# A transformer block on one core: 12 corrections to the list scheduler's order in place of 67

## The chip, the core and the metric

The kernel runs on one core of a Trainium2 chip. The core has five engines, each with an instruction queue of its own that it works through strictly in order: TensorE (PE in the profile; PEld is its loading of weights), VectorE (DVE), ScalarE (ACT), GpSimd (POOL) and SyncE (SP), which here only issues DMA transfers. An instruction that needs the result of another engine waits at the head of its queue, and everything behind it waits too. The metric is the device time of the whole program in microseconds. The kernel before takes 846.68 us, the median of three runs (845.99 to 846.89).

## What is computed

One block of a transformer in float32: LayerNorm, attention over a dilated window, a residual, LayerNorm, a SwiGLU feed-forward network (FFN), a residual. The sizes are 2048 rows (S), model width 640 (D), inner width 1728 (F), and 32 heads of 20. Each position attends to itself and to the seven positions 2, 4, ... 14 before it. Cut to what matters:

```python
def _A_ref(x, wqkv, wo):
    H = 32; Dh = D // H; W, dil = 8, 2
    qkv = (x @ wqkv).reshape(B, S, 3, H, Dh).transpose(2, 0, 3, 1, 4)
    q, k, v = qkv[0], qkv[1], qkv[2]
    idx = jnp.arange(S)[:, None] - (jnp.arange(W) * dil)[None, :]
    mask = idx >= 0
    kg, vg = (the rows idx of k and of v)
    logits = jnp.einsum("bhsd,bhswd->bhsw", q, kg) * Dh ** -0.5
    attn = _softmax(jnp.where(mask[None, None], logits, -1e9))
    o = jnp.einsum("bhsw,bhswd->bhsd", attn, vg)
    return o.transpose(0, 2, 1, 3).reshape(B, S, D) @ wo

def _B_ref(x, w_gate, w_up, w_down):
    return (_silu(x @ w_gate) * (x @ w_up)) @ w_down

h = x + _A_ref(_layernorm(x), wqkv, wo)
h2 = h + _B_ref(_layernorm(h), w_gate, w_up, w_down)
```

## The kernel before

**Tiling.** The 2048 rows are four blocks b of 512, each held as four row tiles j of 128 rows. Heads are taken in four groups g of eight. The FFN's inner width is 14 column tiles i (i0 to i12 of 128, i13 of 64). Products of full float32 accuracy are made of three passes: each operand is split into a high part (a cast on ScalarE) and a low part (a subtraction on VectorE), and TensorE adds high·high, low·high and high·low. So nearly every operand of TensorE first passes through ScalarE and then VectorE.

**Stages.** First come the projections to q, k and v (L552) and the attention of all blocks and groups (L594 loads, L601 and L636 products, L608, L619 and L644 sums on VectorE, L621 the exponential). For each block follow the output projection `wo` (L768 to L805), LayerNorm (L315 to L383, its square root at L373 and what follows it at L374), the FFN with its loads (L845, L851, L858), casts (L846, L847), projections `proj` (L869 to L871), down products `downs` (L880 to L896) and gates (L903 to L915), and `finish` (L1160 to L1182), which adds the down products to the rows `h` and stores them (L1182). The attention of later blocks runs on VectorE while TensorE does FFN and output projection of earlier ones. Blocks 2 and 3 share the products of their FFN through combinations of their columns (L964 products, L1060 to L1130 sums); one factor of it is kept in a tile `kept` (L1130, L1144), which lies in the buffer that held the upper half of `h` before. In the output projection each row tile takes two halves of 320 columns; for blocks 1 and 2 all of them go through a single bank, which ScalarE empties (L802).

**The order.** The program is not executed as it is written. Every piece of work is put on a list by `Plan.add(engine, cost, function, reads, writes, priority)`, 2739 numbered operations in all; `Plan.add` works out from the memory ranges which earlier operations each depends on. `Plan.order` then plans them like a list scheduler: each engine takes the ready operation of the best priority, with estimated costs, and so each operation gets a planned start. The final order is a heap over the dependences with the planned start as its key, to which `SHIFT` adds a correction in microseconds for single operations, by number (L38 and the key in `order`):

```python
key = [(t + SHIFT.get(n, 0.0), n) for n, t in enumerate(start)]
heap, out = [key[n] for n in range(len(ops)) if not left[n]], []
while heap:
    n = heapq.heappop(heap)[1]
    out.append(n)
```

A positive number puts an operation back in its engine's queue, a negative one brings it forward, as far as its dependences let it. Each engine then executes its operations in this order. The waits between engines are put in from the memory ranges. An operation may be several instructions.

**The operations that are spoken of**, with the engine, the line, and the time at which the operation began in the profiled execution of before:

| operation | engine, line | what | at us |
|---|---|---|---|
| 47, 68, 131, 139 | DVE L516, ACT L526, PE L554 | first block: columns of LayerNorm, a cast of weights, two q/k/v products | 14.4, 14.8, 11.6, 13.9 |
| 989 | DVE L374 | LayerNorm's scale after the square root, block 3 | 229.0 |
| 1649, 1650 | PE L871 | FFN block 1, projections of i9, first two steps | 486.9, 488.1 |
| 1662 | PE L896 | FFN block 1, a down product | 494.2 |
| 1453, 1455, 1459 | PE L800 | `wo` of block 2: row tile 2 (two halves), row tile 3 | 500.0, 504.5, 507.4 |
| 1653, 1654 | PE L871 | FFN block 1, further projections of i9 | 502.2, 503.4 |
| 1659, 1679, 1660 | PE L896 | FFN block 1, down products | 532.3 (1659), 506.7 (1660) |
| 820, 825 | DVE L675 | transposes of the attention's result, block 3 | 508.7, 509.1 |
| 1696 | DVE L904 | gate of i11, block 1 | 531.0 |
| 1769, 1771, 1773, 1775 | SP L1182 | stores of block 1's four row tiles | 633.1, 704.4, 676.7, 686.6 |
| 2212 | DVE L1130 | first write of `kept` | 707.0 |

Of the kernel before, what the change touches and what calls it, by code (L numbers as in the profile page):

```python
# [35 lines left out]
PR = {'x': 0.5, 'yst': 8, 'yld': 2, 'wqd': 4, 'wqh': 0.5, 'wql': 4, 'qev': 1, 'kvs': 0.4, 'atl': 1.2, 'exp': 0.5, 'ost': 3, 'wod': 2, 'woh': 8, 'wol': 1.2, 'old': 1.5, 'fld': 4, 'lst': 6, 'wev': 1.5, 'fh': 2.2, 'fl': 8, 'ln1': 8, 't1': 1, 'wo0': 1.2, 'wo': 2.2, 'ln1t': 1.2, 'xb': 0.4, 'tr': 10, 't1t': 2.2, 'ln1d': 0.5, 'hst': 10, 'hld': 10, 'ht': 1, 'hc': 2, 'jd': 3, 'jp': 8, 'js': 4, 'jl': 0.4, 'ja': 0.5, 'jfld': 1.2, 'jfh': 4, 'jfl': 1, 'jhi': 4, 'jmu': 0.4, 'jlo': 0.9, 'jcm': 0.5, 'w3': 1, 'w3e': 8, 'w3o': 0.4, 'w3x': 8, 'w3l': 2.2, 'jy': 6}  # L36

SHIFT = {  # L38
# [8 lines left out]
}  # L47


# [1285 lines left out]
```

## Time and profile before

The profiled execution took 846.34 us; the part that the profile shows, its span, is 844.2 us.

| | us |
|---|---|
| median of the runs | 846.68 |
| profiled execution | 846.34 |
| its span | 844.2 |
| TensorE busy | 837.7 |
| VectorE busy | 706.9 |
| ScalarE busy | 405.0 |
| GpSimd busy | 23.6 |

The granted clock of TensorE is 1.00 in all stretches of the span. A row of a timeline reads: start and length in us, engine, line, instruction, the tile it writes and the tiles it reads with their shapes, and the number of instructions put together in the row; in brackets follows how long the engine stood idle before it and what it waited for. `bank` is an accumulator in PSUM, `fa`, `ra`, `sha` and `shb` are large tiles in SBUF that hold many smaller ones, `acts` holds the gated FFN columns and `h` the rows. SPq is SyncE's queue, where a transfer's issue is shown and not its flight.

### The profile page before, as it was taken

The numbers are of one execution on the slowest core, as the hardware profiler recorded it, in microseconds if no ns is written. First come the engines' busy times: TensorE is split into PE (matmuls) and PEld (weight loads), VectorE is DVE, ScalarE is ACT, GpSimd is POOL, SyncE is SP. The second block draws the span as 40 slices with busy tenths as digits, with TensorE's granted clock in tenths as the row PEclk, the third lists the DMA queues.
The fourth block names the chain that finished last, engine by engine and source line by source line (L and its number), as shares of the span: only waits on it lengthen the run. The fifth ranks groups of instructions, "written<-read, shape, count | busy, mean of one in ns | idle before, by whom it ended". The sixth has DMA issues, their size and how long they took to land.

```text
span 844.2 us, 10772 instructions
## 1 busy us (share of the span) xinstructions
PE 837.7 (99%) x3961; PEld 711.7 (84%) x3961; DVE 706.9 (84%) x841; ACT 405.0 (48%) x674; POOL 23.6 (3%) x33
## 2 busy tenths in 40 slices
PE   9999999999999999999999999999999999999998
PEld 7888888889888888888888898888888887888886
DVE  8899899999998999999999999999434986655652
ACT  6662563245663433875533466555447543333331
POOL 0000000000000100010000000000000000000000
PEclk9999999999999999999999999999999999999999
DMA  8887486567577779567886965876844564454432
GB/s 294 323 298 222 164 274 229 182 216 241 195 255 292 251 255 308 180 216 260 341 289 227 343 234 190 285 274 225 300 164 146 184 229 144 156 169 144 152 115 89
DMA packets 90260, 191.12 MB, mean 226 GB/s; under 512 B 31568, under 2 KB 50896, under 8 KB 89568
## 3 DMA queue, kind: packets, MB, share of 16 engines
q1 hardware_dynamic: 90208, 190.44, 65.8%
q8 instruction: 31, 0.51, 0.3%
q14 instruction: 21, 0.17, 0.1%
HBM read 144.26 MB, written 46.14 MB: 226 GB/s over the span
## 4 chain that ended last, share of the span: by engine, by line
PE 97%; DVE 2%; issue 1%; ACT 0%; DMA 0%; POOL 0%; SPq 0%; POOLq 0%
PE bank L552 25%; PE bank L880 21%; PE bank L869 21%; PE bank L964 17%; PE bank L799 8%; PE bank L986 2%; PE bank L445 1%; DVE fa L608 1%; PE bank L460 1%; DVE acts L915 0%; PE bank L513 0%; PE bank L1166 0%; PE bank L739 0%; DMA out_dram<-h 0%; PE bank L410 0%
## 5 line engine op out<-in xcount | busy, mean ns | idle before, releaser
L869 PE MATMUL bank<-shb,ra 128*128 128x512 f32 x810 | 189.9, 390 | 0.0
L869 PEld LDWEIGHTS bank<-shb,ra 128*128 128x128 f32 x810 | 151.6, 188 | 31.1
L880 PE MATMUL bank<-ra,acts 128*128 128x512 f32 (+1 forms) x662 | 163.1, 389 | 0.0
L880 PEld LDWEIGHTS bank<-ra,acts 128*128 128x128 f32 x662 | 122.5, 188 | 24.5
L552 PE MATMUL bank<-ra,sha 128*128 128x480 f32 x480 | 106.0, 380 | 0.3 <-ACT sha L515 0.3
L552 PE MATMUL bank<-ra,shb 128*128 128x480 f32 x470 | 102.8, 378 | 0.0
L552 PEld LDWEIGHTS bank<-ra,sha 128*128 128x128 f32 x480 | 89.5, 188 | 14.2 <-ACT sha L515 0.8
L552 PEld LDWEIGHTS bank<-ra,shb 128*128 128x128 f32 x470 | 88.0, 188 | 13.2
L636 DVE TENSOR_TENSOR fa<-fa 128x2560 f32<-128x2560 f32 x32 | 90.3, 2823 | 0.8
L601 DVE TENSOR_TENSOR fa<-fa 128x2560 f32<-128x2560 f32 x32 | 90.2, 2820 | 0.4
L608 DVE TENSOR_REDUCE fa<-fa 128x128 f32<-128x2560 f32 x32 | 90.0, 2812 | 0.5
L964 PE MATMUL bank<-shb,ra 128*128 128x512 f32 x360 | 88.3, 391 | 0.8 <-DVE fa L1102 0.8
L557 ACT ACTIVATE st<-bank,fa 128x480 f32<-128x480 f32 x64 | 41.7, 660 | 97.3 <-PE bank L552 86.9
L964 PEld LDWEIGHTS bank<-shb,ra 128*128 128x128 f32 x360 | 67.0, 188 | 14.7 <-DVE fa L1102 1.2
L644 DVE TENSOR_TENSOR fa<-fa 128x1280 f32<-128x1280 f32 (+2 forms) x68 | 75.9, 1116 | 1.6
L1102 DVE TENSOR_TENSOR fa<-bank,fa 128x512 f32<-128x512 f32 x60 | 41.2, 691 | 42.8 <-PE bank L964 41.8
L799 PE MATMUL bank<-ra 128*128 128x320 f32 x480 | 74.6, 309 | 0.0
L799 PEld LDWEIGHTS bank<-ra 128*128 128x128 f32 x480 | 72.3, 188 | 2.2 <-ACT fa L802 0.3
L964 PE MATMUL bank<-ra 128*128 128x512 f32 x288 | 68.4, 390 | 0.0
L964 PEld LDWEIGHTS bank<-ra 128*128 128x128 f32 x288 | 53.9, 188 | 11.7 <-ACT shb L1023 0.4
L846 ACT CAST ra<-fa 128x1280 fp32r<-128x1280 f32 (+1 forms) x38 | 45.8, 1206 | 22.5 <-PE bank L869 16.8
L914 ACT CAST acts<-fa 128x512 fp32r<-128x512 f32 x47 | 29.2, 621 | 54.4 <-DVE fa L904 28.0
(152 smaller groups left out, 842.4 us busy)
## 6 DMA issues: line engine op xcount, KB each, us to landing
fa<-in_ffn_dram SPq DMA_DIRECT2D x46, 960.0 KB, 7.0
ra<-lsc SPq DMA_DIRECT2D x45, 320.0 KB, 4.1
fa<-ksc SPq DMA_DIRECT2D x16, 880.0 KB, 5.3
fa<-vsc SPq DMA_DIRECT2D x16, 880.0 KB, 6.2
ra<-lsc SPq DMA_DIRECT2D x21, 640.0 KB, 5.2
lsc<-ra SPq DMA_DIRECT2D x13, 640.0 KB, 4.4
ksc<-st SPq DMA_DIRECT2D x16, 320.0 KB, 2.7
qsc<-st SPq DMA_DIRECT2D x16, 320.0 KB, 3.0
```

Of the source, the lines that this page charges most:

```text
L552: T.matmul(banks[bk][:, 0:480], l, r_(wq(g, w, c), 480), start=(p, c) == first_mm, stop=(p, c) == last_mm)
L557: P.add("ACT", act(480) + 0.06, lambda bk=bk, j=j: A.activation(stage_t()[:, so : so + 1920].rearrange("p (t j c) -> p t j c", t=3, j=NJ)[ ...
L601: P.add("DVE", dve(2560), lambda: V.tensor_tensor(f(PROD, 2560).rearrange("p (j w c) -> p j w c", j=2, w=W), window(ko, 2 * jp), f(qo + 32 ...
L608: P.add("DVE", dve(2560), lambda: V.tensor_reduce(f(lo + 128 * jp, 128), f(PROD, 2560).rearrange("p (n d) -> p n d", d=DH), axis=AX.X, op= ...
L636: V.tensor_tensor(f(PROD, 2560).rearrange("p (j w d) -> p j w d", j=2, d=DH), bass.AP(tensor=fa[:, vo : vo + 160].tensor, offset=fa[:, vo ...
L644: V.tensor_add(dst(v), v[:, :, 0:m, :], v[:, :, m : 2 * m, :])
L799: T.matmul(banks[bk][:, 0:320], l, r_(m, 320), start=p == 0 and c == 0, stop=p == 2 and c == NC - 1)
L846: P.add("ACT", act(n), lambda: A.copy(r_(gu, n), f(raw, n)), r=[rf(raw, n)], w=[rr(gu, n)], prio=PR["fh"])
L869: T.matmul(banks[bk], r_(gu + 1280 * w + wid * c + col, 128), x2(a, c), start=p == 0 and c == 0, stop=p == 2 and c == NC - 1)
L880: T.matmul(banks[bk][:, lo:hi], l, m, start=first and p == 0, stop=last and p == len(passes) - 1)
L964: T.matmul(banks[bk], r_(ws[w] + 256 * q, 128), x(a, c), start=start and p == n == q == 0, stop=stop and p == 2 and n == len(terms) - 1 an ...
L1102: dv(0, lambda: V.tensor_add(fb(h, dst), banks[bk], fb(h, src)), [pb(bk)] + fr(h, src), fr(h, dst))
```

## The change

The change replaces the table `SHIFT` and nothing else. No operation is added, removed or altered; what differs is the place that operations have in their engines' queues.

```diff
 SHIFT = {
-    10: 0.8, 12: 3.1, 34: 4.5, 68: 1.6, 113: 0.8, 139: -52.8, 322: 21.3, 343: 10.9, 346: 8.4, 403: -3.1, 436:
-    -29.1, 447: 15.5, 453: -103.8, 454: -3.7, 493: -93.9, 550: 3.4, 572: -2.9, 617: -123.3, 713: -1.9, 774:
-    30.6, 793: 9.4, 806: 32.3, 819: 15.7, 855: 9.6, 887: 12.8, 915: 118.8, 989: 9.5, 1249: 24.3, 1421: -13.3,
-    1429: -28.8, 1436: 14.2, 1467: 19.2, 1541: -11.1, 1584: 8.8, 1585: 3.6, 1607: -8.1, 1608: 17.1, 1625: 2.7,
-    1647: 7.2, 1649: -8.4, 1650: -239.9, 1654: -70.9, 1659: 28.8, 1662: -47.2, 1769: 75.2, 1771: 150.6, 1773:
-    120.5, 1775: 133.3, 1777: 5.1, 1812: 13.5, 1838: -17.7, 1842: 15.7, 1870: 15, 1894: 7.6, 1898: 5, 1922: 8.9,
-    1929: 11.8, 1983: 25.7, 2011: -17.9, 2016: 3.5, 2096: 10.5, 2101: 7.3, 2156: 4.9, 2226: 50.2, 2712: 6.8,
-    2713: 6.6, 2733: -52.6
+    10: 0.9, 12: 2.5, 34: 4.5, 47: -27.4, 113: 0.8, 131: -5.8, 2096: 10.8, 2101: 6.1, 2156: 4.1, 2712: 6.9,
+    2713: 6.6, 2733: -78.6
 }
```

Ten keys stand in both tables with nearly the same numbers: 10, 12, 34, 113, 2096, 2101, 2156, 2712, 2713 and 2733. Two are new, 47 and 131. The other 57 operations go back to the place that the list scheduler's planned start gives them. Among them are the four stores of block 1's rows, whose shifts of 75.2 to 150.6 put them back.

## The prediction

> **What bounds the kernel now.** I read the page first, its busy shares and the chain that ended last:
>
> ```profile
> span 844.2 us, 10772 instructions
> ## 1 busy us (share of the span) xinstructions
> PE 837.7 (99%) x3961; PEld 711.7 (84%) x3961; DVE 706.9 (84%) x841; ACT 405.0 (48%) x674; POOL 23.6 (3%) x33
> ...
> PE 97%; DVE 2%; issue 1%; ACT 0%; DMA 0%; POOL 0%; SPq 0%; POOLq 0%
> ```
>
> TensorE (PE) is busy 837.7 of 844.2 us and carries 97% of the chain. The edit changes no instruction, only their order in the engines' queues, so it can win little more than the time in which TensorE stands still now, and it loses wherever it makes TensorE stand still. The table of busy time in stretches of 20 us says where that is (columns: length, then busy time and count of PE, PEld, DVE, ACT and POOL, then clock, DMA share and GB/s):
>
> ```profile
> 0.00:20.00 20.00, 18.22 (x80) 14.62 (x81) 16.23 (x40) 14.33 (x33) 1.17 (x7) 1.00 0.82 288
> ...
> 540.00:560.00 20.00, 19.56 (x93) 15.95 (x92) 19.67 (x26) 11.33 (x20) 0.00 (x0) 1.00 0.82 289
> ...
> 700.00:720.00 20.00, 19.21 (x85) 15.60 (x84) 13.31 (x21) 7.66 (x13) 0.00 (x0) 1.00 0.46 151
> ...
> sum 840.00, PE 836.98 PEld 711.16 DVE 705.97 ACT 405.00 POOL 23.58; mean PE 19.93 PEld 16.93 DVE 16.81 ACT 9.64 POOL 0.56
> ```
>
> Up to 840 us TensorE misses 840 − 836.98 = 3.02 us: 1.78 in the first stretch, 0.44 in that from 540 and 0.79 in that from 700. These three make 3.01, so all other stretches are full. The start aside, the waits that a better order could remove are 0.44 + 0.79 = 1.23 us. In the stretch from 540 VectorE (DVE) is busy 19.67 of 20 us: an instruction of it that is made late there is hardly caught up.
>
> **The change part by part.** Ten of the twelve new shifts repeat an old key at nearly its old value, 47 and 131 are new, and 57 old ones go. Three parts matter: the four stores, the order from 486 to 549 us, and the rest.
>
> *The stores: a gain.* Operations 1769, 1771, 1773 and 1775 (L1182) write the second block's rows, held back to between 633 and 704 us. The last to go is in the chain of waits, around 704 us:
>
> ```profile
> 704.36 1.73 DMA out_dram<-h
> 706.08 0.95 issue
> ```
>
> The timeline names the waiters; in brackets stand the idle time before and what ended it:
>
> ```profile
> 707.03 0.69 DVE L1130 TENSOR_TENSOR kept<-fa 128x512 f32<-128x512 f32 x1 [0.95 <-issue]
> ```
> ```profile
> 710.19 1.20 PE L964 MATMUL bank<-shb,ra 128*128 128x512 f32 x4 [0.79 <-DVE fa L1102]
> ```
>
> `kept` lies in the buffer that held the upper half of `h`, so its first write (operation 2212) waits until the last store has read `h`. VectorE idles 0.95 us for it, and three microseconds of its queue later TensorE idles 0.79. Without their shifts the stores go out as the rows are finished:
>
> ```profile
> 557.85 2.47 DVE L1174 TENSOR_TENSOR h<-bank,h 128x512 f32<-128x512 f32 x4
> ```
>
> That is from 558.5 to 560.3. Operation 2212 then moves 13 places up VectorE's queue, where its 0.69 us fits into the idle 0.91 of this row:
>
> ```profile
> 693.79 0.69 DVE L1102 TENSOR_TENSOR fa<-bank,fa 128x512 f32<-128x512 f32 x1 [0.91 <-PE bank L964]
> ```
>
> The gain lies between 0.79 (TensorE's idle time) and 0.95 (VectorE's whole wait, if the matmuls around it are stretched too). I take 0.9, nearer the chain's figure.
>
> What the stores meet at their new place: each is 128 rows of 640 floats, 0.33 MB, so 1.31 MB together. The table by single microseconds (last two columns DMA share and GB/s):
>
> ```profile
> 560.00:561.00 1.00, 1.00 (x6) 0.81 (x6) 1.00 (x2) 0.83 (x2) 0.00 (x0) 1.00 0.33 136
> 561.00:562.00 1.00, 1.00 (x6) 0.84 (x5) 0.96 (x2) 0.17 (x1) 0.00 (x0) 1.00 0.17 67
> 562.00:563.00 1.00, 1.00 (x7) 0.81 (x6) 0.58 (x1) 1.00 (x1) 0.00 (x0) 1.00 0.00 0
> 563.00:564.00 1.00, 1.00 (x6) 0.84 (x5) 0.96 (x2) 0.34 (x2) 0.00 (x0) 1.00 0.12 31
> ...
> 566.00:567.00 1.00, 1.00 (x6) 0.84 (x5) 1.00 (x3) 0.50 (x1) 0.00 (x0) 1.00 1.06 443
> ```
>
> At 443 GB/s, the rate at 566, they need 3.0 us. From 560 to 564 the DMA engines are free for 4 − (0.33 + 0.17 + 0 + 0.12) = 3.38 us, so they fit into a hole. Behind them in SyncE's queue stands a load, whose median time to land and whose first possible reader are these (SyncE's timeline, the page's DMA part, TensorE's timeline):
>
> ```profile
> 562.96 0.33 SPq L851 DMA_DIRECT2D ra<-lsc  x1
> ```
> ```profile
> ra<-lsc SPq DMA_DIRECT2D x21, 640.0 KB, 5.2
> ```
> ```profile
> 570.52 1.98 PE L964 MATMUL bank<-shb,ra 128*128 128x512 f32 x8
> ```
>
> It lands at 568.2 and is read at 570.5 or later, 2.3 us of slack. I cost this at nothing; without the hole it would be 3.0 − 2.3 = 0.7 us.
>
> *The order from 486 to 549: a loss.* The second block's FFN tiles i9 to i12 (L869 projections, L880 down products) alternate on TensorE with the third block's output projection (L799). The latter has one bank: each half row waits until ScalarE (ACT) has emptied the bank of the half before (L802); then VectorE adds the row (L805), and LayerNorm runs on both. The rows, one fence for each engine's timeline:
>
> ```profile
> 497.70 1.61 DVE L805 TENSOR_TENSOR h<-h,fa 128x640 f32<-128x640 f32 x1 [0.94 <-ACT fa L802]
> ```
> ```profile
> 501.27 0.58 ACT L903 ACTIVATE fa<-bank 128x512 f32<-128x512 f32 x1
> 501.87 1.28 ACT L373 ACT_TABLE_LOAD   x1
> 503.16 0.30 ACT L373 ACTIVATE fa<-fa 128x2 f32<-128x2 f32 x1
> 503.37 0.40 ACT L802 COPY fa<-bank 128x320 f32<-128x320 f32 x1
> ```
> ```profile
> 502.21 2.45 PE L869 MATMUL bank<-shb,ra 128*128 128x512 f32 x10
> 504.50 2.36 PE L799 MATMUL bank<-ra 128*128 128x320 f32 x15
> ```
>
> Two projection steps, 1653 and 1654 (the 2.45 us), stand between the halves 1453 and 1455 and cover the eviction that ends at 503.77. In the new order 1654 follows 1455, so half of the cover goes, 1.2 us; and 1662, a down product of 0.7 us (three matmuls; a row below), moves from before 1453 to behind 1459. So 1455 would be ready at 504.50 − 1.2 − 0.7 = 502.6. Its eviction stands behind gate L903, the square root's table load and the square root; if they keep their times, TensorE waits 503.8 − 502.6 = 1.2 us. But 1649 and 1650, another 2.4 us of projections, also move back, so the row before is projected earlier, VectorE's 0.94 of idle time before 497.70 goes, and ScalarE's queue runs up to 0.8 us sooner: a wait of 0.4. The next half, 1459, has its eviction behind LayerNorm's L331, moved up here, and behind exp's table load; 1654 and the products 1659 and 1660 (1.2 + 0.7 + 0.7 = 2.6 us) now stand ahead of it as cover. I put it at nothing, and at the worst at one table load of 1.28. Together 0.4 to 2.5; I take 0.8, the middle of the first wait, since the second has its cover.
>
> The Trainium skill has a rule that speaks against this: "ScalarE: Activation LUTs", section "What ACT_TABLE_LOAD costs", adds a drain of about 1.38 us to each load of 1.28. Here the load starts at 501.87, right behind the gate's end at 501.85, and the square root 1.29 us later, so the rows show no drain; by the page the eviction would be 1.4 us later and the sum 1.4 higher.
>
> Later in this part the down products 1659 and 1679 move in front of the projections of i11:
>
> ```profile
> 529.61 2.88 PE L880 MATMUL bank<-ra,acts 128*128 128x512 f32 x12
> ```
> ```profile
> 531.00 0.68 DVE L904 TENSOR_TENSOR fa<-bank,fa 128x512 f32<-128x512 f32 x1
> ```
> ```profile
> 548.04 0.69 DVE L908 TENSOR_TENSOR fa<-bank,fa 64x512 f32<-64x512 f32 x1
> ```
> ```profile
> 548.79 0.44 PE L410 MATMUL bank<-fa 128*128 128x128 f32 x2 [0.44 <-DVE fa L908]
> ```
>
> The projections of i11 end at 529.6, where the products begin. Twelve matmuls take 2.88 us, so two products of three add 1.4, and with the 0.8 from above they end at 531.8. VectorE's gate (1696) at 531.00 then waits 0.8, and VectorE carries most of it to L908 at 548.04, for which TensorE already waits 0.44. TensorE is itself 0.8 late by then, which covers nearly all. I take 0.3 more; the bounds are −0.4, that wait gone, and 0.8. This part: 0.8 + 0.3 = 1.1, from 0.4 − 0.4 = 0 to 2.5 + 0.8 = 3.3.
>
> *The rest.* LayerNorm's 989 (L374), at 229 us now, moves seven places up VectorE's queue, to before the row at 220.71, and needs the square root below:
>
> ```profile
> 220.71 2.83 DVE L636 TENSOR_TENSOR fa<-fa 128x2560 f32<-128x2560 f32 x1
> ```
> ```profile
> 221.04 0.29 ACT L373 ACTIVATE fa<-fa 128x1 f32<-128x1 f32 x1
> ```
>
> VectorE waits from 220.7 to 221.3, 0.6 us, with the attention's products behind it. Its later columns for TensorE come at about 240. I take 0.1, bounds 0 and 0.6. The moves at the start (47, 68, 131, 139) lie within the 1.78 us lost there; I take 0, bounds ±0.3. The others (loads issued sooner, casts and evictions some places apart, swaps at 372, at 425 to 480 and at 560 to 690) stand where TensorE's stretches are full, and each puts back by one neighbour's length an operation that is not in the chain. Zero, bounds −0.1 and one VectorE instruction, 0.7. If that cover is gone, they cost the 0.7.
>
> *The sum.* The profiled execution's own time is 846.34 us, 0.34 below the median of the runs, 846.68. 846.34 − 0.9 + 1.1 + 0.1 = 846.64; with the same 0.34, 847.0.
>
> **The rivals.**
>
> *Only the stores count.* The new waits at 486 to 549 are all covered, since each row is projected sooner. For it: that TensorE shows no wait there now, with the same evictions. Against it: 1455 loses 1.9 us of cover. 846.68 − 0.9 = 845.8.
>
> *Slower: VectorE's lateness holds the output projection.* Transposes 820 and 825 now stand ahead of L374 in VectorE's queue, so LayerNorm's scale is late, ScalarE's L331 waits for it, and the eviction of the only bank waits behind L331 and a table load. Then the upper bounds of that part come due: 846.68 − 0.9 + 0.1 + 3.3 = 849.2, with the 0.7 of the rest 849.9. It decides from new waits of 2.6 us (1.7 for the threshold below and 0.9 for the stores' gain). For it: VectorE's 19.67 of 20. Against it: the 2.6 us of cover ahead of 1459.
>
> *The stores give nothing.* `kept` finds another late wait at 691, or the stores push the loads by 0.7: 846.68 + 1.1 + 0.1 = 847.9, or 848.6. Against it: the hole and the slack.
>
> *A table load with a drain.* One uncovered drain on top of the forecast, 847.0 + 1.4 = 848.4. Against it: no gap in the rows.
>
> *A gain.* All 1.23 us of waits go and nothing comes: 845.4; with the start's 0.3 and the rest's 0.1, 845.0.
>
> **How the numbers follow.** 0.2% of the time, 1.7 us, is about what a measurement of this kernel can tell from no change, so the bounds are 845.0 and 848.4. The forecast (846.2 to 848.2) has 0.36, the stores alone 0.17, the slower mechanism 0.33, the stores giving nothing 0.06, the drain 0.02, the gain 0.06. Slower is 0.33 + half of the 0.06 + half of the 0.02 = 0.37; faster the lower end of the gain, 0.04; the same 0.59. The range goes from a little below the stores alone, 845.5, into the slower mechanism, 849.5; it leaves out the gain's 0.06 and the 0.1 or so of that mechanism beyond.
>
> **What the changed profile would show.** Right: L1182 near 560 us, no idle time before the first `kept`, a full stretch from 700; TensorE below 20.00 between 480 and 520 with waits at L799 ended by ScalarE's L802; L904 near 531 later and L410 near 549 still waiting for L908. Wrong: full stretches from 480 to 540, a wait for a load near 570, or time lost in a stretch that I cost at nothing, those from 60 to 480 above all.

## The result and the profile after

The changed kernel takes 844.72 us, the median of 11 runs (844.35 to 845.0), beside 846.39 us for the kernel before on the same chip (11 runs); the ratio is 0.9978, with a 95% interval of 0.9969 to 0.9987. That is 1.9 us less, 1.1 to 2.6 by the interval; by the medians 1.7. The prediction was 847.0 with a range from 845.5 to 849.5: it had the wrong sign and missed its range. The profiled execution took 845.0 us, its span 843.0, against 846.34 and 844.2 before.

The page of the changed kernel, its busy shares and its chain:

```profile
span 843.0 us, 10782 instructions
## 1 busy us (share of the span) xinstructions
PE 837.8 (99%) x3961; PEld 712.0 (84%) x3961; DVE 705.1 (84%) x841; ACT 406.5 (48%) x674; POOL 24.8 (3%) x33
...
PE 99%; ACT 0%; POOL 0%; DVE 0%; issue 0%; POOLq 0%
```

TensorE's work is what it was, 837.8 us beside 837.7; VectorE's share of the chain has gone from 2% to 0%, and the DMA no longer stands in it. In the table by stretches of 20 us (columns as in the prediction):

```profile
0.00:20.00 20.00, 18.25 (x79) 14.85 (x80) 15.95 (x38) 14.30 (x33) 1.17 (x7) 1.00 0.81 283
...
480.00:500.00 20.00, 20.00 (x112) 17.99 (x111) 19.83 (x19) 11.87 (x24) 2.62 (x2) 1.00 0.72 255
500.00:520.00 20.00, 20.00 (x110) 17.99 (x110) 19.72 (x23) 13.20 (x22) 0.00 (x0) 1.00 0.70 212
520.00:540.00 20.00, 20.00 (x91) 16.53 (x91) 16.49 (x20) 11.77 (x19) 2.03 (x2) 1.00 0.70 238
540.00:560.00 20.00, 20.00 (x94) 16.46 (x94) 19.48 (x26) 11.75 (x21) 0.00 (x0) 1.00 0.79 263
...
700.00:720.00 20.00, 20.00 (x90) 16.54 (x89) 12.74 (x20) 7.46 (x13) 0.00 (x0) 1.00 0.45 145
```

Both holes of before, 0.44 in the stretch from 540 and 0.79 in that from 700, are gone, and the expected new ones between 480 and 560 did not come.

The stretches count TensorE as busy where matmuls follow each other slowly. A finer measure is used from here on: **lost time**, worked out from the trace as the distance between the starts of successive matmuls, less the median distance for their line, added up. Where a matmul is stretched around a wait, that is in it; a little below zero means matmuls somewhat closer than the median.

| kernel | time, us | 0 to 20 | 200 to 260 | 480 to 560 | 700 to 720 |
|---|---|---|---|---|---|
| before | 846.39 | 1.26 | −0.15 | 0.93 | 1.06 |
| changed | 844.72 | 1.47 | 0.13 | 0.29 | −0.03 |

Between the two profiled executions the change is +0.28 at 200 to 260, −0.64 at 480 to 560 and −1.09 at 700 to 720: −1.45 together. The first 20 us differ by 0.21 in these two, but no effect of the change can be read from that: in the 11 profiled executions, here and below, that share the old start the figure lies anywhere from 1.08 to 1.83.

### The profile page after: what moved, and what is told of

It reads as the page before. It is cut to its first block, busy times and chain, and to the rows that moved or that the text cites. A ratio compares the mean times of both kernels' runs of the same rounds, so it can differ in the third digit from the quotient of the medians.

```text
span 843.0 us, 10782 instructions
## 1 busy us (share of the span) xinstructions
PE 837.8 (99%) x3961; PEld 712.0 (84%) x3961; DVE 705.1 (84%) x841; ACT 406.5 (48%) x674; POOL 24.8 (3%) x33
## 4 chain that ended last, share of the span: by engine, by line
PE 99%; ACT 0%; POOL 0%; DVE 0%; issue 0%; POOLq 0%
PE bank L546 25%; PE bank L874 22%; PE bank L863 22%; PE bank L958 18%; PE bank L793 8%; PE bank L980 2%; PE bank L439 1%; PE bank L454 1%; PE bank L507 0%; PE bank L404 0%; PE bank L1160 0%; PE bank L733 0%; ACT sha L509 0%; POOL ra L1194 0%; DVE h L1168 0%
## 5 line engine op out<-in xcount | busy, mean ns | idle before, releaser
L793 PE MATMUL bank<-ra 128*128 128x320 f32 x480 | 74.6, 309 | 0.0
L793 PEld LDWEIGHTS bank<-ra 128*128 128x128 f32 x480 | 72.3, 188 | 2.2 <-DVE ra L711 0.2
L908 ACT CAST acts<-fa 128x512 fp32r<-128x512 f32 x47 | 29.1, 620 | 50.7 <-DVE fa L898 25.5
```

Source lines behind the costliest of these rows:

```text
L793: T.matmul(banks[bk][:, 0:320], l, r_(m, 320), start=p == 0 and c == 0, stop=p == 2 and c == NC - 1)
```

## The experiments

All are tables `SHIFT`, but for one; the other kernels' lines are numbered 6 to 9 lower than those of before, since their table is shorter (L796 or L793 is L802 of before). "Before" is the kernel before, run on the same chip beside each group; its median there was 846.39 to 846.53 us. The changed kernel was run beside the first group alone, so a time "above the changed kernel" compares two chips and is good to about 0.1 us at best. Differences of half a microsecond are hardly clear of the intervals of the times; for them the lost time of each run's one profiled execution decides.

**The stores alone, and the changed kernel without them.**

```diff
 (from the kernel before)
-    1769: 75.2, 1771: 150.6, 1773: 120.5, 1775: 133.3
```

> The kernel before with the four shifts of the stores (1769, 1771, 1773, 1775) taken out and the other 63 kept. Theory A (the changed kernel's gain has two sources, the stores and the block at 486 to 549 us): VectorE's wait before the first kept goes, TensorE's last matmul comes 1.1 us sooner, the span falls from 844.2 to 843.1 and the time by 1.1; the 0.6 us that TensorE loses at 549 stays. Rival B (the whole gain is the stores'): the time falls by 1.6 to 1.9 and the span to 842.6 or below. Rival C (kept finds another late wait): no change.

845.42 against 846.51 us before, ratio 0.9986 (0.9977 to 0.9995): 1.1 us less. The lost time at 700 to 720 falls from 1.06 to −0.03, the 0.94 at 480 to 560 stays.

```diff
 (from the changed kernel)
+    1769: 75.2, 1771: 150.6, 1773: 120.5, 1775: 133.3
```

> The changed kernel with the four old shifts of the stores put back. Theory A: the wait of 0.95 us before the first kept is back, the span is 1.1 above that of the changed kernel, 844.1, and the time 0.5 to 0.8 below the kernel before. Rival B (all of the gain is the stores'): the time of the kernel before, span 844.2 or more, or above it if the block costs something.

846.02 us, ratio 0.9992 (0.9983 to 1.0001), 1.3 above the changed kernel's 844.72; the loss at 700 to 720 is back with 1.03, that at 480 to 560 is 0.29 as in the changed kernel. Theory A holds in both directions: the stores are 1.1 us, and not the whole gain. That the rest gains something without the stores is seen in the lost time; the interval of this run's ratio just reaches 1. In the changed kernel SyncE's timeline and VectorE's show the reason:

```profile
558.00 2.91 SPq L1176 DMA_DIRECT2D out_dram<-h  x4
562.81 0.33 SPq L845 DMA_DIRECT2D ra<-lsc  x1
```

```profile
690.98 0.69 DVE L1124 TENSOR_TENSOR kept<-fa 128x512 f32<-128x512 f32 x1
```

The four stores go out from 558 on, the load behind them 0.15 us sooner than before, and the first write of `kept` (L1124 here) stands at 691 with no idle time before it.

**The block from 486 to 549 us by itself.**

```diff
 (from the kernel before)
-    1429: -28.8, 1436: 14.2, 1467: 19.2, 1649: -8.4, 1650: -239.9, 1654: -70.9, 1659: 28.8, 1662: -47.2
```

> The kernel before with eight shifts taken out that set the order from 486 to 549 us (1429, 1436, 1467, 1649, 1650, 1654, 1659, 1662); the stores stay held back. Theory A: no wait at any half of the output projection, the wait at L410 (549 us) gone, span 0.5 to 0.65 below 844.2, time 0.6 down. Rival D (the prediction's step: the eviction of the bank comes 0.4 to 1.2 us late for 1455, and VectorE's gate at 531 late for L410): time 1.1 up. The wait of 0.79 at 710 stays in both.

847.48 us, 1.0 above before, ratio 1.0013 (1.0005 to 1.0022). Here theory A failed, and the size is the prediction's; but the wait is another. TensorE's timeline, then VectorE's:

```profile
528.18 0.66 PE L401 MATMUL bank<-fa 128*128 128x128 f32 x4 [1.07 <-ACT fa L374]
```

```profile
505.27 0.43 DVE L611 TENSOR_TENSOR fa<-fa 128x256 f32<-128x256 f32 x1
506.84 0.69 DVE L895 TENSOR_TENSOR fa<-bank,fa 128x512 f32<-128x512 f32 x1 [1.14 <-PE bank L860]
507.69 0.83 DVE L796 TENSOR_TENSOR h<-h,fa 128x640 f32<-128x640 f32 x1 [0.16 <-ACT fa L793]
508.52 1.51 DVE L378 STREAM_TRANSPOSE fa<-fa 128x1280 f32<-128x1280 f32 x1
509.95 0.65 DVE L906 TENSOR_TENSOR acts<-fa,acts 128x512 fp32r<-128x512 f32 x1
510.52 0.89 DVE L665 STREAM_TRANSPOSE fa<-fa 128x320 f32<-128x320 f32 x2
511.34 2.78 DVE L592 TENSOR_TENSOR fa<-fa 128x2560 f32<-128x2560 f32 x1
```

No half of the output projection waits. The transposes of LayerNorm's columns (1746, L401 here), which the edit brings forward to 527 us, wait for ScalarE's L374 (L383 of before), which is late because VectorE is: it stood idle 1.14 us at 506 and did the transposes 820 and 825 and the attention's product 838 (L665, L592) only from 510.5 on. In the changed kernel VectorE's timeline is this:

```profile
499.93 0.89 DVE L668 STREAM_TRANSPOSE fa<-fa 128x320 f32<-128x320 f32 x2
500.75 2.77 DVE L602 TENSOR_REDUCE fa<-fa 128x128 f32<-128x2560 f32 x1
...
505.39 2.82 DVE L595 TENSOR_TENSOR fa<-fa 128x2560 f32<-128x2560 f32 x1
508.12 0.68 DVE L898 TENSOR_TENSOR fa<-bank,fa 128x512 f32<-128x512 f32 x1
```

There 820, 825 and 838 stand ahead of the gate L898, and fill the time in which it would wait. They do so because 819, GpSimd's addition on which 820 and 825 depend, has lost its shift of 15.7: no operation can be put in the order before one that it depends on. So 819 was tried.

```diff
 (from the kernel before: the eight of the block, and)
-    819: 15.7
```

> The run with the eight shifts of the block taken out, and 819 (GpSimd's addition, behind which the transposes 820 and 825 and the product 838 stand in the order) taken out as a ninth. Theory G (the block is a loss by itself, and 819 turns it: with it 820, 825 and 838 fill VectorE's idle time at 505 to 508, so that LayerNorm's scale at 525 is 2.7 us sooner and the transposes 1746 don't wait): no wait of TensorE at 528 and none at 549, span 844.1 less 0.5, time 0.6 below the kernel before and 1.6 below the run with eight. Rival H (something else among the 57 turned it): the wait of 1.1 to 1.2 us at 528 stays.

```diff
 (from the changed kernel)
+    819: 15.7
```

> The changed kernel with the old shift of 819 alone put back. Theory G: VectorE's product 838 begins near 511 instead of 505.4, the transposes 1746 of TensorE wait 1.0 to 1.3 us for ScalarE's L383 near 528, and the time is 1.0 to 1.3 above the changed kernel, 845.8. Rival H: the changed kernel's time within 0.2, no wait at 528.

Put back into the changed kernel, 819 costs 1.2 us: 845.93 against 844.72, ratio to before 0.9995 (0.9985 to 1.0004); the lost time at 480 to 560 rises from 0.29 to 1.47. The wait at the transposes is there again, and VectorE's idle time before the gate, 2.02 us:

```profile
527.63 0.66 PE L401 MATMUL bank<-fa 128*128 128x128 f32 x4 [1.02 <-ACT fa L374]
```

```profile
506.35 0.69 DVE L895 TENSOR_TENSOR fa<-bank,fa 128x512 f32<-128x512 f32 x1 [2.02 <-PE bank L860]
```

Taken out beside the block's eight, it brings 846.63 us, 0.8 less than the run with eight when each is set against its own before, and no wait at 527; but only the time of before, ratio 1.0001 (0.9992 to 1.001), not 0.6 below it as expected. Another wait was left, in TensorE's and ScalarE's timelines:

```profile
508.20 1.00 PE L790 MATMUL bank<-ra 128*128 128x320 f32 x5 [0.34 <-ACT fa L793]
```

```profile
505.18 0.92 ACT L322 ACTIVATE fa<-h,fa 128x640 f32<-128x640 f32 x1 [0.73 <-DVE fa L363]
506.12 1.28 ACT L612 ACT_TABLE_LOAD   x1
507.42 0.42 ACT L612 ACTIVATE fa<-fa 128x256 f32<-128x256 f32 x1
507.74 0.41 ACT L793 COPY fa<-bank 128x320 f32<-128x320 f32 x1
```

This is the half 1459, behind LayerNorm's L331 (L322 here) and exp's table load: the very place of the slower rival, with 0.5 us of lost time. VectorE is 0.7 us later there than in the changed kernel.

**819 without the block.**

```diff
 (from the kernel before)
-    819: 15.7
```

> The kernel before with 819 alone taken out. Theory G in its old surroundings: VectorE's 838 starts near 506.5 instead of 509.5, but the row addition L805 then stands behind it at about 510 instead of 507.4, so the bank's next eviction is late and TensorE waits up to 0.6 us at the next half (1461, 512 us), while VectorE is 0.9 us sooner at 549 and the 0.6 lost there goes: time within 0.4 of the kernel before. Rival (819 alone is the gain of this part): 0.6 down without a wait at 512.

846.58 against 846.46 us, ratio 1.0000 (0.9991 to 1.0009). The loss at 549 goes and one of 0.61 us at the half 1461 (513 us) comes. With the stores too:

```diff
 (from the kernel before)
-    819: 15.7, 1769: 75.2, 1771: 150.6, 1773: 120.5, 1775: 133.3
```

> The kernel before with five shifts taken out: the four stores and 819. If the two parts add up, the time is that of the run with 819 alone less 1.1 us: 845.0 to 845.7 where the 0.6 at 549 is lost again at 512, 844.7 where it is not. If five of the 57 removals make the whole change, span 842.6 to 843.0 and the changed kernel's time.

845.33 us, ratio 0.9985 (0.9977 to 0.9994), the stores' 1.1 and nothing else: neither the block nor 819 gains alone.

**What brings VectorE forward.** Before the block, the old shifts of 793 and 1421 make VectorE take operations in an order in which it loses time, 0.4 us at 464 and 0.2 at 480.

```diff
 (from the changed kernel)
+    793: 9.4, 1421: -13.3
```

> The changed kernel with the old shifts of 793 and 1421 put back: two exchanges in VectorE's queue at 464 and 480 us, before the part in question. Theory J (VectorE has to reach that part 0.6 us sooner, and these two exchanges bring it there, because VectorE no longer idles before 1598 and before 1421): VectorE is 0.5 to 0.6 us later from 484 on, the eviction 1456 comes late by 0.3 to 0.5 for the half 1459 (508 us), and the time is 0.3 to 0.5 above the changed kernel. Rival (the wait at 508 has another cause): the changed kernel's time within 0.2, no wait at L799.

845.16 us, 0.44 above the changed kernel, ratio 0.9983 (0.9974 to 0.9991); the intervals of the two overlap, and the trace decides. The lost time at 480 to 560 is 0.61 in place of 0.29, 0.21 of it at the half 1459. The profile's list of waits does not name it, since it shows only as stretched matmuls.

```diff
 (from the kernel before: the eight of the block, 819, and)
-    793: 9.4, 1421: -13.3
```

> The kernel before with eleven shifts taken out: the eight of the block, 819, and now 793 and 1421. Theory J: the wait of 0.5 us at 1459 that the run with nine has goes, no wait of TensorE from 480 to 560 is left, and the time is 0.6 to 0.7 below the kernel before. Rival: the time of the run with nine.

845.98 against 846.53 us, ratio 0.9991 (0.9982 to 1.0000): 0.55 less, at the edge of what the times can tell, and no wait at L799. The lost time at 480 to 560 falls from 0.93 to 0.46. With the stores:

```diff
 (from the kernel before: those eleven, and)
-    1769: 75.2, 1771: 150.6, 1773: 120.5, 1775: 133.3
```

> The kernel before with fifteen shifts taken out: those eleven and the four stores. If these are the whole change, the time is the changed kernel's, 844.7, or up to 0.2 below it, since the 0.2 that TensorE loses at 241 there does not come; span 842.3 to 843.0 depending on the start. If more of the 57 takes part, 0.4 or more above.

844.96 us, ratio 0.9982 (0.9973 to 0.9991), beside the changed kernel's 0.9978 (0.9969 to 0.9987). So 15 of the 57 shifts make the change, as far as the times can tell. The traces show two small things that the other 42 do, which nearly cancel: this run still loses about 0.19 us at 554, where the changed kernel loses nothing, and it does not lose the 0.28 at 200 to 260. What removes the loss at 554 was not looked for. One of the ten repeated keys, 2733, has a clearly different number in the changed kernel (−78.6 in place of −52.6), but the time from the start of the last matmul to the end of the span is 3.76 us before and after.

**The prediction's own step: the cover of 1455.** The first run moves the cover behind and leaves the rest; the second puts the two projections back ahead.

```diff
 (from the kernel before)
-    1654: -70.9, 1662: -47.2
```

> The kernel before with only 1654 and 1662 taken out of the table: these two matmul groups go behind 1455 and 1459, but 1649 and 1650 stay ahead of the third block's output projection, so that its rows come no sooner. Theory A (the cover does matter, and is only replaced in the changed kernel by ScalarE's queue running 2.2 us sooner): TensorE waits 0.9 to 1.2 us at the half 1455 for ScalarE's L802 at 503.8, 0.6 of which it would have waited at 549 anyway, so the time is 0.3 to 0.6 up. Rival E (the eviction is covered whatever the order): no wait at L799, no change.

846.29 us, ratio 0.9998 (0.9989 to 1.0007): no change, and no listed wait at the output projection, as the rival had it. That is not because the cover never counts: 1455 began at 503.07, without a wait, but the eviction ahead of it ended at 502.88 and not at 503.8, since 1662 behind also brought the row before 0.56 us sooner, and ScalarE 0.9 us. ScalarE's timeline:

```profile
500.97 1.28 ACT L364 ACT_TABLE_LOAD   x1
502.27 0.30 ACT L364 ACTIVATE fa<-fa 128x2 f32<-128x2 f32 x1
502.47 0.41 ACT L793 COPY fa<-bank 128x320 f32<-128x320 f32 x1
```

The half 1453 was stretched instead, 2.63 us from 499.45 where the trace of before has 2.36, a loss that only takes the place of one at 549 (0.22 there, 0.60 before).

```diff
 (from the changed kernel)
+    1649: -8.4, 1650: -239.9
```

> The changed kernel with the old shifts of 1649 and 1650 alone: these two projection groups go back ahead of the third block's output projection. Theory A (moving them back is what lets ScalarE's queue run 2.2 us sooner and so saves 1455 its wait): ScalarE's sqrt in this part runs near 503 instead of 500.9, TensorE waits about 0.5 us at 1455 for L802, and the span is 0.3 to 0.5 above the changed kernel's 843.0. Rival E (the order of these two does not matter): the same span within 0.1.

845.11 us, 0.4 above the changed kernel, ratio 0.9986 (0.9977 to 0.9995), which overlaps the changed kernel's interval; the lost time at 480 to 560 is 0.62 in place of 0.29. The span is equal, 843.0, only because its first 20 us lost 0.2 less. ScalarE's square root ran at 502.5, 1.6 us later, and TensorE lost 0.23 us just before the half 1455 at 503.17. So the mechanism is there, with half the expected size.

**GpSimd beside VectorE.**

```diff
-                        G.tensor_add(v[:, :, 0, :], v[:, :, 0, :], v[:, :, 1, :])
+                        if b < 3:
+                            G.tensor_add(v[:, :, 0, :], v[:, :, 0, :], v[:, :, 1, :])
```

> The kernel before without GpSimd's addition L664 in the fourth block (three of the twelve; the sum over the last two window positions is left out there). Theory F (VectorE's two-input operations are slowed by a GpSimd addition beside them): L805 near 497.7 takes 0.82 instead of 1.61 us, L915 near 534.9 takes 0.68 instead of 1.89, VectorE reaches L908 at 548 sooner, and of the 0.6 us that TensorE loses at 549 at most 0.2 are left; span 843.6 to 843.8. Rival (those two rows are long for another reason): the same lengths, span 844.2.

This kernel leaves out the addition in the fourth block, three of the twelve, and so the part of the result that it adds. One run, 845.51 against 846.4 us. VectorE's and TensorE's timelines:

```profile
497.61 0.82 DVE L797 TENSOR_TENSOR h<-h,fa 128x640 f32<-128x640 f32 x1 [0.96 <-ACT fa L794]
...
534.85 0.69 DVE L907 TENSOR_TENSOR acts<-fa,acts 128x512 fp32r<-128x512 f32 x1 [0.52 <-ACT acts L906]
```

```profile
548.10 0.38 PE L401 MATMUL bank<-fa 128*128 128x128 f32 x2
```

Both rows have their short length, VectorE runs 1.29 us sooner from 536 on, and TensorE's wait at 549 is gone. At 531.5 VectorE was only 0.09 us ahead of before, so what the first row saved had been used up by then, and the 1.2 us are the second row's. In the kernel before, the GpSimd addition beside the gate's L915 was what caused that wait:

```profile
534.94 1.89 DVE L915 TENSOR_TENSOR acts<-fa,acts 128x512 fp32r<-128x512 f32 x1 [0.52 <-ACT acts L914]
```

In the changed kernel the gate's L904 of 531 comes 1.16 us later and GpSimd's addition 1.48. L915 (L909 here) now begins before GpSimd does and keeps its short length, and the addition falls beside a sum with one input, which keeps its length too:

```profile
535.50 0.68 DVE L909 TENSOR_TENSOR acts<-fa,acts 128x512 fp32r<-128x512 f32 x1
536.10 2.81 DVE L602 TENSOR_REDUCE fa<-fa 128x128 f32<-128x2560 f32 x1
```

```profile
535.72 0.51 POOL L656 TENSOR_TENSOR fa<-fa 128x1 f32<-128x1 f32 x1 [36.60 <-DVE fa L595]
536.19 1.57 POOL L658 TENSOR_TENSOR fa<-fa 128x640 f32<-128x640 f32 x1
```

Here it is GpSimd that is held up: its small subtraction ahead of the addition, 0.19 us before, takes 0.51 and ends just behind L909.

**What the change costs.**

```diff
 (from the changed kernel)
+    403: -3.1, 989: 9.5
```

> The changed kernel with the old shifts of 989 and 403, which set VectorE's and ScalarE's order around 221 us. Theory A: VectorE no longer waits for the square root at 221, TensorE runs 0.2 to 0.26 us sooner from 242 on and the span is 842.75. Rival (the 0.2 is a difference of two executions at the start): the span stays within 0.1 of 843.0.

844.62 us, ratio to before 0.9979 (0.9969 to 0.9988). The lost time at 200 to 260 falls from 0.13 to −0.11, so the step costs 0.2 us in the trace; in the times, 0.1 below the changed kernel, it does not stand out. With the old start as well (10, 12, 34, 68, 113 and 139 as before, 47 and 131 out):

> As the run with 989 and 403 put back, and the start's table of the kernel before as well (10, 12, 34, 68, 113, 139 with their old values, 47 and 131 out). Theory A: TensorE is 0.2 us sooner at 30 us and 0.45 sooner at 242; all of it reaches the end, span 842.5, time 0.45 below the changed kernel. Rival: VectorE is not sooner at 548, TensorE waits there again and the gain shrinks to 0.2 or less.

844.48 us, ratio 0.9978 (0.9970 to 0.9987). Its first 20 us lost 1.08, those of the run without the old start 1.09. No effect of the start shows. Both are at the changed kernel's time within the intervals; none is shown to beat it.

## Why the prediction was wrong

**The bound named the right waits and was too small.** TensorE's work did not change, and the two waits that the prediction counted as the most that could be won, 1.23 us, are the ones that went; with the stretched matmuls around them they were 0.64 + 1.09 = 1.73 us. What came is nearest to the rival "A gain", that all waits go and nothing comes; it had a chance of 0.06, and even its lower end, 845.0, is above the 844.72 measured.

**The stores: right, a little small.** 0.9 was forecast; 1.1 came in the trace and in the run with the stores alone, 1.3 in the run without them, since the stretch around the wait counts. The stores met the hole in the DMA's work; the load behind them landed at 567.2, 4.4 us after its issue, and no wait of TensorE shows near 570.

**The step that failed is the block, "0.8 + 0.3 = 1.1, from 0.4 − 0.4 = 0 to 2.5 + 0.8 = 3.3".** It measured −0.64. Of its parts:

- *1455 waits 0.4 to 1.2 us.* It does not wait. ScalarE's queue "runs up to 0.8 us sooner" was the mistake: it ran 2.2 us sooner. ScalarE's timeline, then TensorE's, with 1455 in the second row:

```profile
499.64 1.28 ACT L367 ACT_TABLE_LOAD   x1
500.94 0.30 ACT L367 ACTIVATE fa<-fa 128x2 f32<-128x2 f32 x1
502.23 0.43 ACT L796 COPY fa<-bank 128x320 f32<-128x320 f32 x1 [1.00 <-PE bank L793]
```
```profile
502.03 1.32 PE L863 MATMUL bank<-shb,ra 128*128 128x512 f32 x5
503.19 2.36 PE L793 MATMUL bank<-ra 128*128 128x320 f32 x15
```

  The eviction now waits 1.00 us for TensorE and ends at 502.66, half a microsecond ahead of 1455 at 503.19. I had counted VectorE's idle time of 0.94 before L805, but not that L805 itself gets shorter, 0.82 in place of 1.61 us, when it runs ahead of GpSimd's addition, nor that two exchanges at 464 and 480 us bring VectorE 0.6 us forward, of which 0.4 are left at 493, since it was 0.2 behind before them. 0.94, 0.79 and 0.4 make nearly all of the 2.2.
- *1459 waits nothing.* True of the changed kernel, by 0.4 us of slack. The slower rival was a real mechanism: its wait shows with 0.5 us in the run with the block and 819, and with 0.2 where 793 and 1421 are put back.
- *820 and 825 ahead of L374 make LayerNorm late* (the slower rival). They do, by 0.8 us beside the run with 819 put back (from the start of the L789 before it, 6.44 us against 5.67), but in the changed kernel ScalarE's L331 does not wait for it. What counts is the other side: they and 838 fill VectorE's idle time, and where they stand behind, VectorE's product is 5.4 us later and the time 1.2 us longer. I had seen in them only something that stands in LayerNorm's way, and not looked at what VectorE did while it waited for the next gate.
- *L904 at 531 is 0.8 late and carries it to 548.* It was 1.16 late; VectorE did not carry it, since the 0.52 us that it idled before L915 went and L915 took 0.68 in place of 1.89 us. L908 (L902 here) came 0.39 sooner, and TensorE's wait at 549 is gone, which was the lower bound of that step and not its value. VectorE's timeline, then TensorE's:

```profile
547.65 0.69 DVE L902 TENSOR_TENSOR fa<-bank,fa 64x512 f32<-64x512 f32 x1 [0.28 <-ACT fa L901]
```
```profile
548.70 0.38 PE L404 MATMUL bank<-fa 128*128 128x128 f32 x2
```

**The rest.** VectorE's wait for the square root was 1.45 us in place of 0.6, since 989 moved past one product (0.82 us) more than the prediction had it, and it cost 0.2 in place of 0.1:

```profile
222.03 0.17 DVE L361 RECIPROCAL fa<-fa 128x1 f32<-128x1 f32 x1 [1.45 <-ACT fa L367]
```

The swaps at 425 to 480, put at nothing, were wrong by 0.3 us in the lost time and 0.4 in the times, those of 793 and 1421: what hid them was VectorE's slack, which the block uses up.

**The sum of the parts.** −1.09 − 0.64 + 0.28 = −1.45 in the trace, and −1.7 by the medians; the interval, 1.1 to 2.6 us, holds both. What makes up the 0.2 between them stays open.

The Trainium skill's rule on a drain behind a table load ("ScalarE: Activation LUTs", section "What ACT_TABLE_LOAD costs") does not hold in these rows: the square root begins 1.30 us after the load did, at 499.64 and 500.94, as it did by 1.29 before; no such drain shows, and the change has as many table loads as before, 34.

## What to carry to other kernels

When an order is changed, walk the queue of the engine that has least slack as a whole: an operation moved ahead costs nothing if it fills a wait, and a part that loses alone can win beside another. When a step's cost hangs on operations that "keep their times", follow their chain back to its own releasers before pricing it; here it came 2.2 us sooner. Tables of single corrections aren't additive: eight shifts cost 1.0 us, a ninth that alone does nothing took 0.8 of that away, and with two more the eleven won 0.55.

## What the runs showed of the hardware

In the rows of this case, GpSimd's addition (128x640, 1.57 us alone) and VectorE's operations with two inputs from SBUF hold each other up for as long as the first one runs. Before, L915, which takes 0.68, began 0.23 us after an addition that ran from 534.71 to 536.28, and took 1.89, to 0.55 us after its end:

```profile
534.71 1.57 POOL L664 TENSOR_TENSOR fa<-fa 128x640 f32<-128x640 f32 x1
```

The order can be the other way too: in the changed kernel the addition began 0.01 us behind the end of L805, met L789, and both were long:

```profile
497.09 2.03 POOL L658 TENSOR_TENSOR fa<-fa 128x640 f32<-128x640 f32 x1
```

```profile
497.00 3.00 DVE L783 TENSOR_TENSOR ra<-fa,ra 128x512 fp32r<-128x512 f32 x3
```

Those three L789 take 1.62 us in the run without the addition. The sum L608, with one input, is not held up (2.81 us beside the addition). The Trainium skill's "SBUF — State Buffer", section "SBUF: two separate sides", says the same: the pair of ports that VectorE and GpSimd share is locked by one of them for a whole instruction, if VectorE's has two inputs in SBUF and GpSimd's reads it. The rows agree, with 1.2 us for one such meeting, and the run without the addition shows what it was worth: 0.7 us of lost time from 480 to 560 (0.93 to 0.25).
